# Wide one-row projections, statistics by matmul, and an order by longest path in a two-layer decode kernel

## The chip, the cores and the metric

The kernel runs on one core of one Trainium2 chip. The metric is the device time of one execution in microseconds (us). A kernel is timed several times, beside runs of the kernel before on the same chip. Of the kernel before, three runs gave a median of 344.33 us (342.01 to 346.02).

A program on one core also has a slower state in some executions; a run over 1.5% above the fastest of the same kernel is called slow. A median is of all executions, the slow ones too. A ratio is the mean time of one kernel's fast runs over the mean of the other's fast runs of the same rounds, so it is not quite the ratio of the medians that stand beside it. Chips differ by about one per cent (the kernel before had medians of 343.6 to 347.5 us in the calls below), so runs of different calls are compared by their ratios.

In the profile, PE is TensorE (its matmuls), PEld its weight loads, DVE VectorE, ACT ScalarE, POOL GpSimd and SP the engine that issues DMAs; "L439" is line 439 of that run's kernel file, so one place in the code has different numbers in different runs.

## The reference

Eight rows (the batch), one token each, width 448. Two layers, each an attention over the last 1,024 keys of a cache (16 query heads, 8 key/value heads, 256 wide) and an MLP (448 to 1,792 to 448). Both layers use the same cache and the same weights:

```
x = x + A(layernorm(x))      # q = x wq; softmax(q k^T / 16) v; wo
x = x + B(layernorm(x))      # silu(x w1) w2
x = x + A(layernorm(x))
x = x + B(layernorm(x))
```

## The kernel before

The weights stay in SBUF. The keys and values of one row are 16 loads of 512 KB (8.4 MB); they come into 27 slots and serve both layers of their row, so they are read once. A slot gets its next load when layer 2 of its row is done with it. The queries of layer 1 are made for all rows at the start, and the last MLP is done for all rows at the end. In between, each row goes through layer 1, its MLP and the scores of layer 2 on its own. The kernel is a list of tasks. A planner simulates them and fixes the order of each engine before the program is built:

```python
def push(t):                       # next task: smallest prio given by hand
    heapq.heappush(heap, ((t.prio if t.eng != "sp" else -1e9), t.idx, t))
...
def proj(bank_i, col, outs, ins, lhs, rhs, n, fresh=True):    # all projections; one row: n == 1
    for o in outs:
        for i in ins:
            fns.append(lambda e, o=o, i=i: e.matmul(
                bank[bank_i][:, col + (o - outs[0]) * n:col + (o - outs[0] + 1) * n], lhs(o, i), rhs(i), ...))
...
def pv_cols(b, layer, kvh, ...):   # p times V, by columns of V: 16 matmuls into one bank
    c0 = DH + 4 * j
    ... e.matmul(bank[ob][:, c0 + 2 * a:c0 + 2 * a + 2], vs[...], pT_sb[...])
    dve(... oT_dst <- bank[ob][:, c0:c0 + 4] * rl_sb ...)     # DVE reads that bank
...
def layer1(b):
    # 16 DVE transposes of keys, scores, softmax, then by turns pv_rows / pv_cols and wo_part
def layer2(b):
    # chain(b): w1, silu, w2, statistics, wq;  then scores, softmax, pv_rows of layer 2
```

`[...]` and `...` are cuts.

## Time and profile before

The median is 344.33 us; the profiled execution has a span of 343.4 us. The next lines are from its page: busy time by engine, then the span in 40 slices (one digit is the busy share in tenths; PEclk is the granted TensorE clock in tenths of full speed), the DMA queues (packets, MB, share of the 16 engines), the chain of waits (SPq is the sequencer of SP, which issues the loads), and two groups of instructions (count, busy us, mean ns of one, then the idle time of the engine before them and what ended it).

```profile
PE 232.8 (68%) x5966; PEld 173.1 (50%) x5966; DVE 169.6 (49%) x510; ACT 46.4 (14%) x163; POOL 10.5 (3%) x22
...
PE   1052435677488886796779668777877688887584
...
PEclk9999999998555556559655965686568555655565
DMA  7999999999950699049925991799089808100000
...
q1 hardware_dynamic: 49936, 77.68, 66.0%
q8 instruction: 47, 0.77, 0.9%
...
PE 51%; DVE 13%; SPq 12%; DMA 9%; issue 8%; ACT 7%; DVEq 0%; ACTq 0%
...
L439 PE MATMUL bank<-oT,wo_sb 128*128 128x1 bf16 (+1 forms) x1152 | 32.2, 165 | 4.5 <-issue 4.5
...
L630 PE MATMUL bank<-pT_sb,slot 128*128 128x2 bf16 x512 | 17.6, 164 | 11.9 <-DVE oT L636 7.7
```

The reader is to see four things. No engine is full, so the time is a chain of waits, of which PE is half. After the first quarter PE runs at half clock for about three quarters of the time (mean clock 0.62 over 100 to 280 us). (The trace has no clock records of about the first 80 us; the 9s there are a filling and not a measurement: 64 score matmuls at 76.5 us take 3.58 us, as long as in half-clock stretches.) DMA pauses between rows, so the loads are not the limit. And "issue" is 8% of the chain: time for which the profile shows no cause. About half of it is stops in which PE stood still for 0.4 to 3.0 us; the rest is in pieces below 0.3 us. The stops stand beside packets of the queue named "instruction".

The row is the unit in what follows. I measure it from the start of a row's w2 projection to that of the next row. In the windows view, a line is the window, its length, the busy time of each engine, the clock, the DMA share and GB/s. Two rows of the kernel before:

```profile
142.34:175.22 32.88, 25.53 (x688) 19.39 (x688) 20.90 (x59) 5.22 (x19) 1.23 (x2) 0.66 0.73 258
...
208.09:241.87 33.78, 26.11 (x687) 19.59 (x688) 19.46 (x58) 5.32 (x19) 1.23 (x2) 0.65 0.70 251
```

From the timeline of PE (start, duration, instruction group):

```profile
178.01 1.42 PE L439 MATMUL bank<-xbt,wq_sb 112*128 112x1 bf16 x48
...
180.54 1.88 PE L543 MATMUL bank<-slot,qbd 128*8 128x256 bf16 x32
```

48 one-column matmuls take 1.42 us, 30 ns each with the pipeline's own latency of some 0.15 us in it; the 32 score matmuls take 1.88 us here, at half clock. At full clock they take 1.04 to 1.10 us.

### The profile page before, as it was taken

The numbers are of one execution on the slowest core, as the hardware profiler recorded it, in microseconds if no ns is written. First come the engines' busy times: TensorE is split into PE (matmuls) and PEld (weight loads), VectorE is DVE, ScalarE is ACT, GpSimd is POOL, SyncE is SP. The second block draws the span as 40 slices with busy tenths as digits, with TensorE's granted clock in tenths as the row PEclk, the third lists the DMA queues.
The fourth block names the chain that finished last, engine by engine and source line by source line (L and its number), as shares of the span: only waits on it lengthen the run. The fifth ranks groups of instructions, "written<-read, shape, count | busy, mean of one in ns | idle before, by whom it ended". The sixth has DMA issues, their size and how long they took to land.

```text
span 343.4 us, 12913 instructions
## 1 busy us (share of the span) xinstructions
PE 232.8 (68%) x5966; PEld 173.1 (50%) x5966; DVE 169.6 (49%) x510; ACT 46.4 (14%) x163; POOL 10.5 (3%) x22
## 2 busy tenths in 40 slices
PE   1052435677488886796779668777877688887584
PEld 0051125654277545664755466456654665476363
DVE  5069200467656644565647556635663566212313
ACT  2000000201102020203020302121112111211111
POOL 0001000000000100001000000100010000000000
PEclk9999999998555556559655965686568555655565
DMA  7999999999950699049925991799089808100000
GB/s 200 263 407 379 361 312 271 403 339 368 404 165 4 211 388 371 19 132 380 389 89 188 388 380 31 252 398 333 5 274 403 307 4 261 49 4 4 0 4 3
DMA packets 49989, 78.50 MB, mean 229 GB/s; under 512 B 2176, under 2 KB 40848, under 8 KB 49488
## 3 DMA queue, kind: packets, MB, share of 16 engines
q1 hardware_dynamic: 49936, 77.68, 66.0%
q8 instruction: 47, 0.77, 0.9%
q14 instruction: 6, 0.05, 0.0%
HBM read 77.67 MB, written 0.01 MB: 226 GB/s over the span
## 4 chain that ended last, share of the span: by engine, by line
PE 51%; DVE 13%; SPq 12%; DMA 9%; issue 8%; ACT 7%; DVEq 0%; ACTq 0%
PE bank L439 22%; PE bank L543 11%; PE bank L602 8%; SPq L417 7%; DMA slot<-in_A_k_cache_dram 5%; DMA w_sb<-in_B_w_dram 4%; PE bank L630 4%; SPq L405 2%; ACT e_sb L566 2%; SPq L411 2%; ACT o_sb L609 2%; DVE mseg L552 1%; PE bank L571 1%; DVE slot L782 1%; PE bank L522 1%
## 5 line engine op out<-in xcount | busy, mean ns | idle before, releaser
L782 DVE STREAM_TRANSPOSE slot<-slot 128x512 uint32<-128x512 uint32 x128 | 87.4, 698 | 13.9 <-DMA slot<-in_A_k_cache_dram 11.9
L543 PE MATMUL bank<-slot,qbd 128*8 128x256 bf16 x1024 | 58.9, 401 | 13.1 <-DVE slot L782 8.8
L543 PEld LDWEIGHTS bank<-slot,qbd 128*8 128x8 bf16 x1024 | 28.9, 113 | 30.4 <-DVE slot L782 9.5
L602 PE MATMUL bank<-slot,pT_sb 128*2 128x256 bf16 x768 | 36.4, 347 | 3.5 <-DMA slot<-in_A_v_cache_dram 3.5
L439 PE MATMUL bank<-oT,wo_sb 128*128 128x1 bf16 (+1 forms) x1152 | 32.2, 165 | 4.5 <-issue 4.5
L439 PEld LDWEIGHTS bank<-oT,wo_sb 128*128 128x128 bf16 x1152 | 31.4, 103 | 4.7 <-issue 4.7
L439 PE MATMUL bank<-xbt,wq_sb 112*128 112x1 bf16 x1024 | 32.1, 165 | 2.1 <-ACT xbt L695 2.1
L439 PEld LDWEIGHTS bank<-xbt,wq_sb 112*128 112x128 bf16 x1024 | 29.8, 104 | 6.2 <-issue 3.4
L630 PE MATMUL bank<-pT_sb,slot 128*128 128x2 bf16 x512 | 17.6, 164 | 11.9 <-DVE oT L636 7.7
L602 PEld LDWEIGHTS bank<-slot,pT_sb 128*2 128x2 bf16 x768 | 18.8, 99 | 12.8 <-DMA slot<-in_A_v_cache_dram 5.2
L630 PEld LDWEIGHTS bank<-pT_sb,slot 128*128 128x128 bf16 x512 | 15.6, 99 | 13.5 <-issue 10.0
L439 PE MATMUL bank<-xbt,w_sb 112*128 112x1 bf16 (+1 forms) x504 | 16.4, 166 | 6.7 <-issue 4.3
L439 PEld LDWEIGHTS bank<-xbt,w_sb 112*128 112x128 bf16 x504 | 15.0, 104 | 7.6 <-issue 4.4
L571 PE MATMUL bank<-ident,e_sb 128*128 128x128 bf16 x64 | 7.8, 259 | 14.9 <-ACT e_sb L566 14.9
L552 DVE TENSOR_REDUCE mseg<-bank 128x2 f32<-128x512 f32 x16 | 11.0, 687 | 13.2 <-PE bank L543 13.0
L511 POOL TENSOR_TENSOR qbd<-q1s,mask 128x256 bf16<-128x256 bf16 x16 | 9.8, 612 | 244.5 <-PE bank L543 220.7
L439 PEld LDWEIGHTS bank<-hT,w_sb 128*128 128x128 bf16 x448 | 12.7, 104 | 7.9 <-DVE hT L688 7.0
L439 PE MATMUL bank<-hT,w_sb 128*128 128x1 bf16 x448 | 13.4, 165 | 4.7 <-DVE hT L688 4.3
L636 DVE TENSOR_TENSOR oT<-bank,rl_sb 128x4 bf16<-128x4 f32 x32 | 5.2, 162 | 22.0 <-PE bank L630 22.0
L615 DVE TENSOR_TENSOR oT<-bank,rl_sb 128x16 bf16<-128x16 f32 x24 | 4.9, 204 | 22.1 <-PE bank L611 21.5
L571 PEld LDWEIGHTS bank<-ident,e_sb 128*128 128x128 bf16 x64 | 4.4, 112 | 20.7 <-ACT e_sb L566 18.9
L609 ACT ACTIVATE o_sb<-bank 128x256 bf16<-128x256 f32 x24 | 9.2, 383 | 41.4 <-PE bank L602 41.4
(108 smaller groups left out, 156.8 us busy)
## 6 DMA issues: line engine op xcount, KB each, us to landing
slot<-in_A_k_cache_dram SPq DMA_DIRECT2D x64, 512.0 KB, 9.5
slot<-in_A_v_cache_dram SPq DMA_DIRECT2D x64, 512.0 KB, 7.8
wq_sb<-in_A_wq_dram SPq DMA_DIRECT2D x4, 896.0 KB, 10.7
wo_sb<-in_A_wo_dram SPq DMA_DIRECT2D x1, 3584.0 KB, 27.4
w_sb<-in_B_w_dram SPq DMA_DIRECT2D x2, 1568.0 KB, 16.3
qbd<-in_A_x_dram SPq DMA_DIRECT2D x1, 7.0 KB
out_dram<-e_sb SPq DMA_DIRECT2D x1, 7.0 KB
```

The source lines that it names most:

```text
L405: dma(lambda e: e.dma_start(slots[s][:, :].rearrange("p (u d) -> p u d", d=DH), A_k_cache[b, kvh, S0:SK, :].rearrange("(p u) d -> p u d", ...
L411: dma(lambda e: e.dma_start(slots[s][:, :].rearrange("v (q n) -> v q n", q=4), A_v_cache[b, g, S0:SK, :].rearrange("(q v uh) d -> v q (uh ...
L417: dma(lambda e: e.dma_start(slots[s][:, :].rearrange("v (j n) -> v j n", j=4), src.rearrange("j (v uh) d -> v j (uh d)", uh=2)), [("slot", ...
L439: fns.append(lambda e, o=o, i=i: e.matmul(bank[bank_i][:, col + (o - outs[0]) * n:col + (o - outs[0] + 1) * n], lhs(o, i), rhs(i), start=( ...
L511: add("pool", lambda e, k2=k2: e.tensor_tensor(qbd[0][:, 4 * k2:4 * k2 + 4, :, :].rearrange("p k c (q r) -> p (k c) q r", r=2), q1s[:, b, ...
L543: fns.append(lambda e, cb=cb, par=par, j=j, kvh=kvh, kv=kv: e.matmul(bank[sc][32 * j:32 * j + 8, k2 * 256:(k2 + 1) * 256], qbd[qi][:, kvh, ...
L552: dve(lambda e: e.tensor_reduce(mseg[ei][:, 0:2], bank[sc][:].rearrange("p (k n) -> p k n", k=2), AX.X, ALU.max, negate=True), bk(sc), [(" ...
L571: pe([lambda e, c=c: e.matmul(bank[lb][:].bitcast(BF16)[:, c * P:(c + 1) * P], e_sb[ei][:, c // 2, c % 2, :], ident[:, :], is_transpose=Tr ...
L602: fns.append(lambda e, q=q, uh=uh, j=j, vv=vv: e.matmul(bank[ob][32 * j:32 * j + 2, k2 * DH:(k2 + 1) * DH], pT_sb[ei][:, k2 * 2 + uh, j * ...
L609: act(lambda e: e.activation(o_sb[oi][:], bank[ob][:, k2 * DH:(k2 + 1) * DH], ACTF.Copy), bk(ob), [("o", oi)], 0.42, prio, "oev")
L630: fns.append(lambda e, a=a, q=q, uh=uh: e.matmul(bank[ob][:, c0 + 2 * a:c0 + 2 * a + 2], vs[:, (2 * q + uh) * DH + a * P:(2 * q + uh) * DH ...
L782: dve(lambda e, v=v: e.transpose(v, v), [("slot", s)], [("slot", s)], 0.68, prio, "KT")
```

## The change

There are three parts and some small ones.

1. Projections of one row move 32 equal columns instead of one (`broadcast_to`), so that TensorE looks busy to its clock control.
2. The sums for layernorm come from matmuls of the bf16 row with ones and with itself, instead of a DVE reduction, an ACT square and a split into two bf16 parts.
3. The order of each engine follows the longest path to the end instead of hand-given priorities, with measured durations and latencies. Softmax and PV of layer 2 then fill gaps of the next row's layer 1.
4. Small moves: three short operations go from DVE to ACT, and `pv_cols` alternates between two PSUM banks, so that PE need not wait until DVE has read the first one.

```diff
+PE_LAT = 0.13
+LOAD_MARGIN = 1.5
...
+        for t in reversed(sorted(tasks, key=lambda t: t.idx)):     # rank: longest path to the end
+            r = 0.0
+            for u in succ[t.idx]:
+                lat = 0.04 if t.eng == u.eng else (PE_LAT + 0.05 if t.eng == "pe" else 0.05)
+                r = max(r, u.rank + lat)
...
-            heapq.heappush(heap, ((t.prio if t.eng != "sp" else -1e9), t.idx, t))
+            heapq.heappush(heap, ((-t.rank if t.eng != "sp" else -1e9), t.idx, t))
...
+    CW = 32
...
+        wide = n == 1
+        n = CW if wide else n
...
-                    bank[bank_i][:, col + (o - outs[0]) * n:col + (o - outs[0] + 1) * n], lhs(o, i), rhs(i),
+                    bank[bank_i][:, col + (o - outs[0]) * n:col + (o - outs[0] + 1) * n], lhs(o, i),
+                    rhs(i).broadcast_to([rhs(i).shape[0], CW]) if wide else rhs(i),
...
-        c0 = DH + 4 * j
+        vb = ob if j % 2 == 0 else LB[layer]
+        c0 = (DH if j % 2 == 0 else C_Q) + 4 * j
...
     def stats1(prio):
-        dve(lambda e: e.tensor_reduce(st[0:CP, 0:1], xbt[0:CP, :], AX.X, ALU.add), ...)
-        act(lambda e: e.activation(junk[0:CP, :], xbt[0:CP, :], ACTF.Square, ..., accum_out=st[0:CP, 1:2]), ...)
-        ...                                          # copy and subtract: split into two bf16 parts
+        fns = [lambda e, c=c: e.matmul(s1, ones_b[0:CP, :], xbt[0:CP, c:c + 1], ...) for c in range(KC)]
+        fns += [lambda e, c=c: e.matmul(s2, xbt[0:CP, c:c + 1].broadcast_to([CP, P]), xbt[0:CP, c:c + 1], ...)
+                for c in range(KC)]
...
+        prio = 100 * b + 170                         # layer 2: softmax and PV
         softmax(b, 1, prio + 2, rs16[b % 2], [("rs16", b % 2)])
```

## The prediction

> **What bounds the kernel now.** The chain of waits gives TensorE 51% of the span, DVE 13%, "issue" 8%; DMA matters only in the head. In the timeline, hT of row 0 is ready at 65 us, of row 1 at 106, of row 7 at 310: the last six rows take 34.0 us each, and 33 us follow. K/V loads (8.4 MB a row at about 390 GB/s, 21.5 us) are not the limit there. A row is one serial chain: w2, wq, layer-2 scores, softmax, PV, then the next row's layer-1 softmax, PV, wo, w1. In it: 32 score or PV matmuls take 1.88 us in stretches at half clock and 1.04 us at full (timeline); layer-2 softmax and PV of row b sit before the layer-1 softmax of row b+1 (row 5: 256.4 to 261.2 us); and TensorE stops 1.4 to 3.0 us about once a row, each stop beside a 16,384-byte instruction packet (47 in the DMA queues).
>
> The Trainium skill, "TensorE: Matmul & The Clock Gate" (The HAM clock gate), says that the clock is half or full, decided by 3.4 us windows of activity. The clock records agree: only 0.5 and 1.0, 3413 ns steps. Counting moved columns per window, full clock follows windows with dense score/PV work (about 3,000 full-array columns); dense one-column projections (over 100 matmuls a window) are always followed by half clock.
>
> **What the change does.**
> 1. Projections move 32 columns. They are spaced 27 ns now (128 in 3.43 us), so 32 columns should fit at no cost even at half clock. About 368 a row add 11,800 columns; a row then has about 28,000, or 3,350 per window over 28 us: just above what seems needed. I expect full clock 65 to 80% of the steady time. The chain has about 3.7 us a row that halving the clock adds; I expect 1.3 us of it left.
> 2. Statistics by matmuls drop the DVE reduce and split and the ACT square, mostly hidden behind w1/wq; perhaps 0.3 us each.
> 3. The order: row b's layer-2 softmax and PV now fill gaps of row b+1's wo part. Removes about 4.7 us a row from the chain, gives back 0.8.
>
> Summing the new chain by hand with the trace's durations: 28.9 us a row at full clock, plus 1.3 for half clock, plus about 1.5 for instruction stops, is 31.7, against 34.0. Head: w1 and w2 land at 58.0 and 62.5 as before, hT of row 0 near 63. The first period falls most, 41 to about 29, because layer-1 scores of row 1 no longer wait behind layer-2 softmax and PV. Tail 33 to 30. 92 + 6*31.7 + 30 = 312. Estimate: 311 us, range 297 to 327. Chances: faster 0.94, same 0.05, slower 0.01.
>
> **What would show it.** Groups: projection matmuls still about 27 ns apart. Clock: above 0.65 over 100 to 300 us, against about 0.61. Timeline: hT to hT about 31.5 us; the pT transposes of layer 1 of row b+1 before those of layer 2 of row b. PV groups 1.04 us more often. Stops of 1.5 to 3 us beside instruction packets remain.
>
> **What would make it wrong.** Wide projections costing more than 27 ns; activity below the threshold, leaving half clock (about 325); instruction stops multiplying because the wo part has over 300 dense matmuls; DVE blocked by a key transpose waiting for a load. Or clock full nearly always and stops hidden: below 300.

## The result, and the profile after

The changed kernel is correct and took 330.31 us (329.66 to 331.38, four runs), beside 344.27 us for the kernel before (342.01 to 346.02). The ratio is 0.9601, with a 95% interval of 0.9539 to 0.9663. It is faster, as forecast, but 19 us slower than the estimate of 311, and above the range of 297 to 327. The same views of its profile:

```profile
PE 223.5 (68%) x6082; PEld 166.3 (50%) x6082; DVE 147.3 (45%) x426; ACT 50.7 (15%) x163; POOL 10.5 (3%) x22
...
PE   1052363675866759778759787979597779798583
...
PEclk9999999996975985779656975587769676996755
DMA  7999999999875596829871998298729881900000
...
q8 instruction: 47, 0.77, 0.9%
...
PE 48%; SPq 18%; DVE 12%; ACT 9%; issue 8%; DMA 4%; ACTq 0%
...
L453 PE MATMUL bank<-oT,wo_sb 128*128 128x32 bf16 (+1 forms) x1152 | 38.0, 180 | 3.5 <-issue 2.9
...
L645 PE MATMUL bank<-pT_sb,slot 128*128 128x2 bf16 x512 | 18.0, 164 | 5.5 <-issue 3.9
```

The clock did rise and the wait of `pv_cols` for DVE (7.7 us before, L630) is gone. But PE is still busy for only 68% of the span. Rows 1, 5 and 6 in the windows view:

```profile
100.89:134.87 33.98, 25.29 (x700) 18.55 (x700) 17.02 (x49) 5.80 (x19) 1.22 (x2) 0.75 0.69 230
...
234.88:268.78 33.90, 25.93 (x699) 18.67 (x700) 16.91 (x48) 5.80 (x19) 1.23 (x2) 0.75 0.71 240
268.78:297.83 29.05, 24.41 (x699) 18.36 (x700) 15.12 (x44) 5.80 (x19) 0.00 (x0) 0.83 0.42 137
```

Rows 1 to 5 take as long as before, 33 to 34 us; row 6 takes 29.05 us. Here is the forecast in its own parts, beside what the timeline shows:

| part | forecast, us | measured, us | difference |
|---|---|---|---|
| head, to w2 of row 0 | 63 | 63.8 | +0.8 |
| first period (row 0 to row 1) | about 29 | 37.1 | +8.1 |
| six periods | 6 x 31.7 = 190 | 196.9 | +6.7 |
| tail after the last | 30 | 31.8 | +1.8 |

The six periods hold five of 33.6 us on average, 1.9 us too long each, and row 6, 2.7 us shorter than forecast. What sets row 6 apart is that its loads end inside it (DMA share 0.42, no load left for a next row) and that no stop of PE above 0.3 us falls into it. The waits view of PE (line, what it waited for: us in total, times, longest) tells how much the stops grew. First the kernel before, then the one after; all lines that end in "issue" are shown:

```profile
PE bank L439 <- issue: 10.2, 6, 3.0
...
PE bank L543 <- issue: 2.3, 2, 1.6
```

```profile
PE bank L453 <- issue: 10.7, 8, 2.9
...
PE bank L645 <- issue: 3.9, 3, 1.8
...
PE bank L616 <- issue: 3.8, 2, 2.5
...
PE bank L557 <- issue: 2.6, 3, 1.6
...
PE bank L659 <- issue: 1.7, 1, 1.7
```

12.5 us in all before, 22.7 after. One such stop, from the timeline of PE in row 1:

```profile
120.34 0.60 PE L453 MATMUL bank<-oT,wo_sb 128*128 128x32 bf16 x18
...
123.80 0.27 PE L453 MATMUL bank<-oT,wo_sb 128*128 128x32 bf16 x4 [2.86 <-issue]
```

PE stops in the middle of one projection, whose inputs are all there, for 2.86 us. In the DMA records a packet of 16,384 bytes on the instruction queue starts at 121.32 us and takes 1.09 us; PE goes on 1.39 us after its end. This holds for every stop: the 17 of after and the 8 of before each end 1.27 to 1.60 us after such a packet has ended. Of the other waits of PE in these two traces (72 and 134), 2 and 6 end between 1.2 and 1.7 us after one. So what ends a stop is the arrival of instructions. Row by row, the stops of 0.5 us or more add up to 4.7 us in row 0 and 3.4, 4.3, 2.7, 2.3 and 3.3 us in rows 1 to 5, a mean of 3.2; the kernel before had 2.1 in the same rows. The forecast had put in 1.5.

The Trainium skill says where these packets come from ("Runtime: NRT & Kernel Launch", section "Instruction fetch mechanics"): instructions come in blocks of 16 KiB, 256 instructions, and the next block is fetched while the present one runs; the cost of crossing from block to block it calls "mostly hidden". The trace agrees on the size: 6,082 matmuls and 6,082 weight loads over 47 packets are 259 a packet. It does not agree that the cost is hidden: the stops above end when a block has come.

So the first theory was: the hand sum of the row is right, and what is missing are stops of TensorE for instructions, which come while K/V loads run. Rivals: the widened projections cost time after all; the new order is worth less than its 3.9 us a row; the new statistics lengthen the chain; the stops belong to certain instructions and not to block boundaries.

### The profile page after: what moved, and what is told of

It reads as the page before. It is cut to its first block, busy times and chain, and to the rows that moved or that the text cites. A ratio compares the mean times of both kernels' runs of the same rounds, so it can differ in the third digit from the quotient of the medians.

```text
span 329.6 us, 13056 instructions
## 1 busy us (share of the span) xinstructions
PE 223.5 (68%) x6082; PEld 166.3 (50%) x6082; DVE 147.3 (45%) x426; ACT 50.7 (15%) x163; POOL 10.5 (3%) x22
## 4 chain that ended last, share of the span: by engine, by line
PE 48%; SPq 18%; DVE 12%; ACT 9%; issue 8%; DMA 4%; ACTq 0%
PE bank L453 22%; PE bank L616 11%; PE bank L557 8%; SPq L429 7%; SPq L417 7%; DVE slot L795 5%; DMA slot<-in_A_k_cache_dram 4%; ACT e_sb L580 4%; PE bank L645 3%; PE bank L585 2%; DVE mseg L566 2%; SPq L423 1%; DVE qbd L540 1%; ACT o_sb L623 1%; PE bank L625 1%
## 5 line engine op out<-in xcount | busy, mean ns | idle before, releaser
L795 DVE STREAM_TRANSPOSE slot<-slot 128x512 uint32<-128x512 uint32 x128 | 80.4, 681 | 14.2 <-DMA slot<-in_A_k_cache_dram 14.2
L557 PE MATMUL bank<-slot,qbd 128*8 128x256 bf16 x1024 | 50.8, 346 | 20.4 <-DVE slot L795 10.1
L616 PE MATMUL bank<-slot,pT_sb 128*2 128x256 bf16 x768 | 40.2, 330 | 11.7 <-DMA slot<-in_A_v_cache_dram 4.4
L557 PEld LDWEIGHTS bank<-slot,qbd 128*8 128x8 bf16 x1024 | 25.2, 98 | 34.5 <-DVE slot L795 11.4
L453 PE MATMUL bank<-oT,wo_sb 128*128 128x32 bf16 (+1 forms) x1152 | 38.0, 180 | 3.5 <-issue 2.9
L453 PE MATMUL bank<-xbt,wq_sb 112*128 112x32 bf16 x1024 | 32.6, 186 | 6.6 <-issue 4.5
L616 PEld LDWEIGHTS bank<-slot,pT_sb 128*2 128x2 bf16 x768 | 14.9, 87 | 19.2 <-issue 10.4
L453 PE MATMUL bank<-hT,w_sb 128*128 128x32 bf16 x448 | 13.3, 187 | 13.7 <-DVE hT L701 13.7
L453 PE MATMUL bank<-xbt,w_sb 112*128 112x32 bf16 (+1 forms) x504 | 17.4, 181 | 3.9 <-issue 3.4
L453 PEld LDWEIGHTS bank<-hT,w_sb 128*128 128x128 bf16 x448 | 12.5, 103 | 14.5 <-DVE hT L701 14.5
L566 DVE TENSOR_REDUCE mseg<-bank 128x2 f32<-128x512 f32 x16 | 11.1, 692 | 17.9 <-PE bank L557 17.9
L580 ACT ACTIVATE e_sb<-bank,mb 128x256 bf16<-128x256 f32 x16 | 6.7, 470 | 75.2 <-DVE mb L573 75.2
```

The lines of the kernel that those rows point to most:

```text
L453: fns.append(lambda e, o=o, i=i: e.matmul(bank[bank_i][:, col + (o - outs[0]) * n:col + (o - outs[0] + 1) * n], lhs(o, i), rhs(i).broadcas ...
L557: fns.append(lambda e, cb=cb, par=par, j=j, kvh=kvh, kv=kv: e.matmul(bank[sc][32 * j:32 * j + 8, k2 * 256:(k2 + 1) * 256], qbd[qi][:, kvh, ...
L566: dve(lambda e: e.tensor_reduce(mseg[ei][:, 0:2], bank[sc][:].rearrange("p (k n) -> p k n", k=2), AX.X, ALU.max, negate=True), bk(sc), [(" ...
L580: act(lambda e, k2=k2: e.activation(e_sb[ei][:, k2, :, :].rearrange("p uh (jj ul) -> p uh jj ul", ul=4), bank[sc][:, k2 * 256:(k2 + 1) * 2 ...
L616: fns.append(lambda e, q=q, uh=uh, j=j, vv=vv: e.matmul(bank[ob][32 * j:32 * j + 2, k2 * DH:(k2 + 1) * DH], pT_sb[ei][:, k2 * 2 + uh, j * ...
L795: dve(lambda e, v=v: e.transpose(v, v), [("slot", s)], [("slot", s)], 0.7, prio, "KT")
```

## The experiments

Eighteen kernels ran. "After" means the changed kernel, "before" the one before it. The expectations name theories by letters: A is the prediction's own accounting, in which each part is worth what the prediction gave it; the other letters are the rivals, as each text puts them. Each of the 18 passed the comparison with the reference, also those that are wrong, which the tolerance doesn't notice.

### Taking the change apart

**The projections one column wide again.**

```diff
-    CW = 32
+    CW = 1
```

> The changed kernel with the projections moved back to 1 column; order, statistics and everything else as changed. Theory A (the wide projections did what they were costed for, and what is missing is elsewhere: stops of TensorE beside instruction packets): mean granted clock falls from 0.75 a row to 0.6 or less, each row gets 1.5 to 2 us longer, time about 341 to 344 us, stops as before. Rival B (the wide projections buy nothing, that is where the forecast gain is missing): same time within 2 us (329 to 332), whatever the clock does.

Measured: 341.04 us, ratio 0.9957 (0.9876 to 1.0039). The clock in rows 1 to 6 falls to 0.50 to 0.55; one of these rows, and the 48 projection matmuls of after that are read below:

```profile
170.45:204.06 33.61, 28.42 (x700) 19.77 (x700) 17.01 (x48) 5.80 (x19) 1.22 (x2) 0.55 0.73 243
```

```profile
278.04 1.40 PE L453 MATMUL bank<-xbt,wq_sb 112*128 112x32 bf16 x48
```

In the new kernel the wide projections are worth 11 to 12 of the 14 us (10.7 by the medians, (0.9957 - 0.9601) x 344.3 = 12.3 by the ratios). That the wide matmuls themselves are free is seen in the timelines: 48 of them take 1.40 us in row 6 of after (29 ns each), where 48 narrow ones took 1.42 us above. The stops were 14.5 us and not "as before" (22.7): that part of the expectation missed. The skill's "TensorE: Matmul & The Clock Gate", Part 1, subsection "Wait — 56ns, not 53.3ns?", states a floor of about 25 ns from start to start for small matmuls; this case shows 25 ns at full clock and 27 at half clock within long groups, at 1 as at 32 columns (medians of before, after and this run).

**The old order, with all else of the change.**

```diff
-SEM_LAT = {"pe": 0.05, ...}; PE_LAT = 0.13; LOAD_MARGIN = 1.5
+SEM_LAT = {"pe": 0.06, ...}; PE_LAT = 0.0; LOAD_MARGIN = 0.0
-    heapq.heappush(heap, ((-t.rank if t.eng != "sp" else -1e9), ...
+    heapq.heappush(heap, ((t.prio if t.eng != "sp" else -1e9), ...
-        prio = 100 * b + 170
```

> The changed kernel with the queue order by the old hand-given priorities and old latencies; wide projections and new statistics stay. Theory A (the order pays, about 4 us a row off the chain before stops): time 338 to 346 us, rows 2 to 6 about 33 to 35 us, layer-2 softmax before the next row's layer-1 softmax again. Rival C (the order gave back what it took, for instance by key transposes that wait for loads at the head of DVE's queue): 328 to 334 us.

Measured: 332.49 us, ratio 0.9697 (0.9618 to 0.9776). The order is worth about 1% of the time (0.9697 against 0.9601, with intervals that overlap), and nothing like the 3.9 us a row of the forecast. In the two traces it does not shorten the rows at all: the six periods average 31.7 us in the old order and 32.8 in the new one. What it wins lies elsewhere: w2 of row 0 starts at 63.8 us instead of 68.0, the first period is 37.1 us instead of 39.3, the tail 31.8 instead of 34.0. The stops of the old order were 17.6 us. The time is that of rival C; its reason, transposes that wait for loads, is not tested here. (The plan keeps the new durations of operations; only priorities, latencies and margin are old.)

**The old statistics in the new kernel.** The edit puts `stats1` and `stats8` of before back.

> The changed kernel with the statistics of before (reduce, square and split on DVE and ACT, two small matmuls). Costed at 0.3 us twice a row: 7 rows * 0.6 = 4 us slower, about 334 us. If the statistics by matmuls are worth nothing: 330 us.

Measured: 329.55 us, ratio 0.9606 (0.9536 to 0.9675). The new statistics are worth nothing that these runs can see.

**Wide projections alone in the kernel before.** The edit is the part of the diff on `CW`, with the outputs laid out 32 apart.

> The kernel before with only the projections widened to 32 columns. Theory A: clock of the rows rises from 0.61 to 0.7 or more, about 1.5 us a row saved, 332 to 337 us, instruction stops of 1.4 to 3 us once a row remain. Rival B (wide projections buy nothing): 342 to 346 us.

Measured: 342.63 us, ratio 0.9958 (0.9864 to 1.0052). The time is that of rival B. Alone, the part that was worth 11 us in the new kernel is worth almost nothing.

**One bank for `pv_cols` in the new kernel, and two banks in before with wide projections.**

```diff
 # in after
-        vb = ob if j % 2 == 0 else LB[layer]
-        c0 = (DH if j % 2 == 0 else C_Q) + 4 * j
+        vb = ob
+        c0 = DH + 4 * j
```

> The changed kernel with the four column-form PV groups of a row back in one PSUM bank, as before (the change lets every second one use the bank of layer 1's softmax sums). Found after the first runs: in the kernel before, each of these groups waits 0.35 us for DVE to read the last one; four a row are 1.4 us, 9 to 10 us over 7 rows. Theory F (this unnamed part of the change carries much of the gain in a row by priorities): in the long-path order other work fills these waits, so here it costs less, 1 to 6 us: 331 to 336 us. If it is worth nothing anywhere: 330 us.

> The kernel before with the wide projections and the column-form PV groups in two banks in turn, nothing else. Theory F: 1.4 us a row off the wide one (342.6 us): 331 to 336 us, close to the changed kernel in old order (332.5 us). If the gap between those two comes from the statistics or from copies moved to ACT: 340 to 344 us.

Measured: 332.02 us for the first, ratio 0.9585 (0.9511 to 0.966), and 339.15 us for the second, ratio 0.9694 (0.9597 to 0.9791; two fast runs, 334.73 and 338.49). The kernel before had 347.54 us, so the ratios count. In the new order a second bank brings nothing: with one bank, too, the trace has no wait of these matmuls for DVE, where before had 7.7 us. In the old order it makes the step from 0.9958 to 0.9694. That is the same as the new kernel in the old order (0.9697): wide projections and two banks are the whole gain there.

**Two banks alone in before.**

> Before, with the two PSUM banks of the column-wise PV alone (projections stay one column wide, old order). The PV groups waited 0.35 us each for DVE, four to a row. If that wait alone explains what the two banks brought beside wide projections (ratio 0.996 to 0.969), the ratio here is 0.965 to 0.980. If both are needed, because a row gets full clock only with wide projections and without pauses, the ratio is 0.985 to 1.005.

Measured: 340.52 us, ratio 0.9883 (0.9745 to 1.002), with only two fast runs. It lies nearer to the second expectation, but its interval reaches into the first one too. The product of the two parts alone is 0.9958 x 0.9883 = 0.984, and both together gave 0.969. That fits a gain that needs both, but the intervals are too wide to call it shown.

**Two knobs on the forecast's other terms:** 64 columns for wo and w2, to raise the clock further, and a wider margin for loads in the plan.

```diff
 # a_cx64
-        n = CW if wide else n
+        cw = CX if bank_i == XB and not fresh else CW      # CX = 64
+        n = cw if wide else n
 # a_margin6
-LOAD_MARGIN = 1.5
+LOAD_MARGIN = 6.0
```

> The changed kernel with wo and w2 moving 64 columns (wq and w1 stay at 32). At full clock 64 columns should still fit the 27 ns between matmuls, at half clock they need 53 ns. If the clock is held by moved columns in a window: granted clock of rows 1 to 5 rises from 0.74 to 0.85 or more and the time falls to 322 to 327 us. If the time at half clock doubles without raising the clock: 335 us or more.

> The changed kernel, planned with 6 us in place of 1.5 us of margin between a load and the key transposes that read it: the three transposes that stand among wo's copies in DVE's queue move behind w2's start. Rival C (transposes waiting for loads at the head of DVE's queue hold up wo): rows 1 to 5 get shorter by 0.5 us or more, 325 to 328 us. Theory A: no gain, 329 to 333 us, since eleven transposes then stand on the chain after w2.

Measured: 335.94 us, ratio 0.9663 (0.9602 to 0.9725), and 338.38 us, ratio 0.9655 (0.9553 to 0.9757). The 64 columns did raise the clock (0.834 in the profile, against 0.788) and did not make the kernel faster. They were not free: in this trace they stand 53 ns apart at half clock (27 at 32 columns) and 29 to 31 ns at full clock (25), and most of w2, 56 matmuls in a row's chain, ran at half clock. So the run does not tell what the rest of half clock is worth. The margin brought nothing that its two fast runs (333.14 and 337.36) show.

### The stops

**No K/V loads for rows 2 to 7.** Only 8 of the 128 partitions are loaded, so that every load is still issued, waited for and counted by the planner at its full size; the outputs are wrong. The order of all engines is unchanged.

```diff
+        if b >= 2:
+            dma(lambda e: e.dma_start(slots[s][0:8, :]..., A_k_cache[b, kvh, S0:SK, :]...[0:8]),
+                [("slot", s)], W * DH * 2, "slot%d" % s)
+            return
```

> The changed kernel, where the K and V loads of rows 2 to 7 bring only 8 of the 128 partitions (wrong result on purpose; same instructions and order, a sixteenth of the traffic from about 85 us on). Theory A (the missing time is stops of TensorE while its instructions are fetched behind K/V traffic): stops of 0.5 us and more vanish after 100 us, rows 1 to 6 take 29 to 30 us each as the last row does now (29.05), time 305 to 312 us. Rival D (the stops come from the dense matmul stream alone, whatever DMA does): rows stay at 33 us, 328 to 331 us.

> The kernel before with the same cut of the loads of rows 2 to 7 (wrong result on purpose). Theory A: its stops (2.1 us a row in rows 1 to 5) vanish too, rows 1 to 6 at 31 to 33.5 us, time 330 to 336 us; the gap between the two kernels grows from 14 to 22 us or more, which is near what was predicted. Rival D: 342 to 345 us.

Measured: 312.33 us for after without loads, ratio 0.9098 (0.9004 to 0.9192), and 334.2 us for before without them, ratio 0.9735 (0.9637 to 0.9833). No stop of 0.5 us or more is left in either once row 1 is loaded; one of 0.16 us (after) and one of 0.41 us (before) are. All "issue" lines of the waits view, after without loads:

```profile
PE bank L463 <- issue: 2.0, 2, 1.8
...
PE bank L669 <- issue: 1.7, 1, 1.7
```

This is the 311 us of the forecast, almost, though the rows are longer than the 29 to 30 us that theory A gave them. Its six periods average 30.9 us, beside 28.9 + 1.3 = 30.2 in the hand sum without the stops. Against before without loads the change is worth 22 us (334.2 to 312.3); with loads it is worth 14. So a third of what the change wins is given back.

But no load also means that data is never late. The kept traces tell how much that can be: after 90 us DVE waits for keys for 1.1 us in all in after, and PE never for values, so there was hardly any late data to take away. And in the chain that ended last, stops of PE above 0.15 us make up 19.2 us in after and 0.2 us in after without loads, where the spans differ by 18.4 us (329.6 and 311.2). So on the chain the stops account for the difference; this is from one trace each.

**Keeping the traffic, but into a spare buffer.** Small loads carry the data, and the full loads go to three spare tiles which nobody reads.

> As a_noload, but for every small load of rows 2 to 7 a full 512 KB load of the same data goes to one of three scratch tiles that nothing reads (24 slots in place of 27 for room; wrong result on purpose). The traffic is there, the waits for data are nearly gone. Theory A: stops come back beside instruction packets, rows 1 to 5 at 32 to 34 us, time 322 to 330 us. Rival E (rows are slow because DVE and TensorE wait for late K and V data): as fast as a_noload.

Measured: 361.11 us, ratio 1.0519. It meets neither expectation. This run is inconclusive: the spare tiles left room for only 24 slots, and the planner counted the bytes twice, so the order of the engines changed as well. Stops beside instruction packets are back (2.77 us in one row), but the time says nothing.

**Moving the block boundaries.** 64 tiny matmuls in front of everything shift all later instructions within their blocks of 256.

```diff
+    pe([lambda e: e.matmul(bank[YB][0:1, 0:1], ones_b[0:1, 0:1], ones_b[0:1, 0:1], start=True, stop=True)] * 64,
+       ["ones_b"], bk(YB), 2.0, -20, "shift")
```

> The changed kernel with 64 tiny matmuls put in front, while TensorE waits for the first weights anyway: every later instruction stands 128 places further along, so the 16,384-byte instruction blocks end at other places of a row. Theory A: the stops move to other instructions (a stop in wo turns up in PV or w1), their sum a row stays within 2 to 4.5 us; time 326 to 334 us. If the stops belonged to certain instructions of the row, they would stay where they are.

Measured: 328.07 us, ratio 0.9543 (0.9463 to 0.9623), 21.6 us of stops. The stops move to other instructions: row 6, which had one of 0.27 us, now has two (2.25 us together). So they belong to the places of instruction blocks and not to what the instructions do.

**When the packets come.** The trace allows a count without a new run: how many TensorE instructions (matmuls and weight loads) start between one instruction packet and the next. The mean is 248 to 257 in every run, near the 256 of a packet. If each packet came in time, all distances would be about 256. I take the standard deviation over 100 to 285 us, in one trace each. Without loads it is 31 (before) and 32 (after). With them it is 98 and 127, and single packets come up to 544 instructions after the one before. The packet at 121.32 us, beside the stop of 2.86 us shown above, came 510 instructions after the one before: PE had run through two blocks, and stood until 1.39 us after this one had come. So under K/V traffic the packets come late, and a stop follows. The packets themselves take no longer: 1.06 us on average in after and 1.11 us without loads over the same stretch. What is late is their start. What remained open was which property of the traffic does it.

**Half the bytes, and fewer loads in flight.** In the first kernel each load of rows 2 to 7 fetches 64 of the 128 partitions. In the others every load of row 1 and later is complete, but SP waits before each one until the load two (or three, or four) before it has landed. The plan is left alone, so the order of all engines is the same as in after.

```diff
 # a_half: as a_noload above, [0:64] instead of [0:8]
 # a_pace2, a_pace3, a_pace4: in the code that emits the engines' programs; N is 2, 3, 4
+                    if e == "sp" and t.sem.startswith("slot"):
+                        seen.append(t)
+                        if len(seen) > 16 + N:
+                            o = seen[-1 - N]
+                            eng.wait_ge(handles[o.sem], o.val)
```

> After, but the K/V loads of rows 2 to 7 fetch 64 of the 128 partitions (outputs wrong on purpose; order of all engines unchanged). Without these loads the TensorE instruction packets came 256 instructions apart with a standard deviation of 32, and no stop followed; with them the deviation was 127 and the stops took 3.2 us a row. If the amount of traffic makes the packets late, half of it gives stops between none and 3.2 us a row, deviation 40 to 110, and 314 to 324 us. If any traffic is enough, 328 to 332. If what mattered in the run without loads was not traffic but data landing early, stops stay and the time is near 325.

> After, with one more wait in front of each K/V load from row 2 on: the load before the last has landed. So at most two 512 KB loads are in flight; order of all engines unchanged. If packets are late because many loads stand in the DMA engines at once, the deviation of the packet spacing falls below 90 and stops below 1.5 us a row, and the time falls to 318 to 326 unless loads then come late. If two loads keep the engines just as busy for a packet, stops stay at 2.5 to 3.5 us and the time is 328 to 336.

> As the run before with three loads in flight. If the number in flight counts, stops lie between those of two in flight and those of the changed kernel; if it does not, stops of 2.5 to 3.5 us a row and 327 to 333 us.

> After, with at most four 512 KB loads in flight (three gave a ratio of 0.9345, two 1.0447 because keys landed late, no limit 0.9601). If fewer loads in flight is what lets the instruction packets through, four lies between three and no limit: ratio 0.935 to 0.958. If three only happened to shift the stops to a harmless place, four may land anywhere, 0.93 to 0.97.

(The expectations say "from row 2 on" for the second; the wait begins after the first two, three or four loads of the second row, the one numbered 1 here.)

> Before, with at most three loads in flight. Its stops took 2.1 us a row over five rows; without loads it ran at a ratio of 0.9735. If pacing frees the instruction packets here too, the deviation of their spacing falls from 98 below 80 and the ratio is 0.970 to 0.990. If the gain needs the new order, 0.995 to 1.01.

Measured, with the stops ("issue" of PE in the waits view, all lines added up) and the deviation of the packet distance:

| kernel | us | ratio (95%) | stops, us | deviation |
|---|---|---|---|---|
| before | 344.27 | 1 | 12.5 | 98 |
| after | 330.31 | 0.9601 (0.9539 to 0.9663) | 22.7 | 127 |
| after, half the bytes | 320.48 | 0.9298 (0.9200 to 0.9397) | 13.2 (slow) | 86 (slow) |
| after, four in flight | 325.22 | two fast runs: 321.42, 322.47; by hand 0.938 | 13.5 | 119 |
| after, three in flight | 320.20 | 0.9345 (0.9264 to 0.9425) | 4.8 | 70 |
| after, two in flight | 356.39 | 1.0447 (1.0358 to 1.0536) | 1.5 | 50 |
| after, hardly any bytes | 312.33 | 0.9098 (0.9004 to 0.9192) | 3.7 | 32 |
| before, three in flight | 337.88 | 0.9764 (0.9643 to 0.9884) | 5.9 (slow) | 75 (slow) |
| before, hardly any bytes | 334.2 | 0.9735 (0.9637 to 0.9833) | 2.9 | 31 |

Stops and deviation are from one trace each, and two of these traces ("slow") fell in the slow state; a difference of a few microseconds between two sums means little (the kernel with the old statistics has 16.3 us of stops and the same time as after). The record calls the verdicts of these test kernels "unclear", and gives none for four in flight; but all four executions of three in flight (318.2 to 323.3 us) and both without loads (311.5 and 313.1) lie below all four of after (329.7 to 331.4).

Both theories of the traffic fit: with half the bytes there are fewer stops (in a slow trace; the two fast runs, 317.0 and 318.9 us, are faster too), and a limit on the loads in flight lowers them with all bytes moved. The stops fall with that limit step by step, 22.7, 13.5, 4.8 and 1.5 us. With two in flight the stops are nearly gone, but the loads then come late: in that run DVE waits for keys as in the first line below, and in the run with three as in the second (in after it is 14.2 us).

```profile
DVE slot L801 <- DMA slot<-in_A_k_cache_dram: 63.2, 26, 12.2
```

```profile
DVE slot L801 <- DMA slot<-in_A_k_cache_dram: 20.7, 13, 13.3
```

Three in flight is the balance here. It beats both kernels, and "issue" is 4% of its chain where it was 8%. All its "issue" lines in the waits view of PE:

```profile
PE bank L459 <- issue: 1.8, 2, 1.2
PE bank L665 <- issue: 1.2, 1, 1.2
PE bank L651 <- issue: 0.8, 1, 0.8
PE bank L622 <- issue: 0.8, 2, 0.4
PE bank L563 <- issue: 0.2, 1, 0.2
```

Its profile, with the DMA issues (size and median us from issue to landing) of after for comparison in the second fence:

```profile
PE   1042347375696968696979797968778878897583
...
PEclk9999999999598679876675879699697967865955
DMA  7999999979999698988986899599888895600000
...
slot<-in_A_k_cache_dram SPq DMA_DIRECT2D x64, 512.0 KB, 5.3
slot<-in_A_v_cache_dram SPq DMA_DIRECT2D x64, 512.0 KB, 5.4
```

```profile
slot<-in_A_k_cache_dram SPq DMA_DIRECT2D x64, 512.0 KB, 6.7
slot<-in_A_v_cache_dram SPq DMA_DIRECT2D x64, 512.0 KB, 6.3
```

The DMA line no longer falls to 0 to 2 between rows: the same bytes are spread out. In windows, two of its rows and all of its six periods' sum:

```profile
165.21:195.50 30.29, 25.61 (x700) 18.80 (x700) 16.91 (x48) 5.79 (x19) 1.22 (x2) 0.77 0.86 279
195.50:225.09 29.59, 23.94 (x700) 18.14 (x700) 16.96 (x48) 5.80 (x19) 1.23 (x2) 0.87 0.85 276
...
sum 184.10, PE 151.41 PEld 111.77 DVE 99.96 ACT 34.77 POOL 6.13; mean PE 25.23 PEld 18.63 DVE 16.66 ACT 5.79 POOL 1.02
```

184.1 us against 196.9 in after: 12.8 us less in the six periods. The forecast's own sum without stops was 6 x 30.2 = 181. Three in flight was not timed side by side with after; the two are compared by their ratios (0.9345 and 0.9601, whose intervals are apart).

## Why the prediction was wrong, point by point

**The direction was right, the size was not.** Faster was given 0.94, and it is faster; the estimate was 19 us too low.

**"Plus about 1.5 for instruction stops": this step failed.** The mechanism was named, but the term of the sum was mis-sized. It measured 3.2 us in rows 1 to 5 and 4.7 in row 0. The kernel before already had 2.1, and the prediction took less than that instead of more. Take the stops out, and the six periods of after are 196.9 - 16.2 = 180.7 us, beside the 181 of the forecast without stops. Why the stops grew is a reading: a late packet hurts only if PE would otherwise have worked, and in before PE often waited for DVE or ACT anyway. The sums fit that, 12.5 us in before, 14.5 with narrow projections, 17.6 in the old order, 22.7 in after, but each is of one trace, and no run took this by itself. The prediction's list of what would make it wrong had this very point, "instruction stops multiplying because the wo part has over 300 dense matmuls"; dense matmuls alone don't do it, since the same stream without loads has hardly any stop.

**"The first period falls most, 41 to about 29": this failed too.** It fell to 37.1. Stops of 4.7 us fell into it (the prediction does not say how much of its 29 was meant for stops). Beside them, row 1's keys are still arriving (the last one that its scores need lands at 73.9 us, 10 us into the period), and its scores ran at half clock (32 in 1.85 and in 1.88 us); what each of the two cost is not shown. In the run with hardly any bytes from row 2 on, this period was 32.4 us.

**"28.9 us a row at full clock, plus 1.3 for half clock": the sum was right, the split was not.** Row 6, with 0.3 us of stops, took 29.05 us. The rows of the run without loads averaged 30.9 us, and those with three loads in flight 30.7, beside 30.2. But the 1.3 us went with full clock for 65 to 80% of the time, and rows 1 to 5 had it for about half (next but one point). By the prediction's own 3.7 us that would leave about 2.0 us instead of 1.3, so a part of the agreement is luck.

**"32 columns should fit at no cost even at half clock": right.** Spacing stayed at 27 ns at half clock and 25 ns at full clock.

**"About 3,000 full-array columns" a window for full clock: right in direction, too high in result.** The clock of rows 1 to 5 rose from a mean of 0.63 to 0.74 (windows view). As the records hold only half and full, 0.74 is full clock for about half of the time; forecast was 65 to 80%. The Trainium skill, "TensorE: Matmul & The Clock Gate", Part 1: The HAM clock gate, gives two clock levels and windows of 3.4 us of activity; the records here hold only 0.5 and 1.0 and change in steps of 3,413 ns. It gives no measure of activity in columns. That came from the trace of before. Counted again there, the five windows of 3.4 us with 100 or more matmuls of one or two columns are all followed by half clock. The 11 windows that moved over 12,400 columns are all followed by full clock (score and PV matmuls stand four side by side in the array, so this is about 3,100 full-array columns); between 8,800 and 12,400 both occur. The narrow kernel (0.50 to 0.55 in its rows) fits that dense one-column matmuls don't count as busy.

**"Statistics ... perhaps 0.3 us each": wrong in size.** They are worth nothing measurable (0.9606 against 0.9601).

**"The order ... removes about 4.7 us a row ..., gives back 0.8": wrong.** The old order with everything else new is 1% slower, and in the traces its rows are shorter, not longer (31.7 against 32.8 us); the new order wins in the head, the first period and the tail. Part of what the prediction gave to the order may be PV work at half clock, which the wide projections also mend, and so have been counted twice; this is not shown.

**What the prediction left out:** the second bank of `pv_cols`. In the old order it and the wide projections make the whole gain (0.9694). In the new order it brings nothing (0.9585 without it): the wait is gone there with one bank too. The parts of this change are not additive: the wide projections are worth about 12 us in the new kernel and 1.4 us, within the noise, alone. That they work on the same waits of PE is my reading.

**What stays open:** on which DMA engine an instruction packet waits, and behind what, is not in the trace. The Trainium skill ("DMA: Bandwidth & Descriptors", section "Queues, rings and completion order") says that a DMA engine goes round-robin between the queues it has work for, one packet at a time. By that rule alone I would not expect the number of loads behind a queue to matter (this is my inference and not the page's), and it does here; no run here tells why. Nor is it worked out why three in flight removes 17.9 of 22.7 us of stops and wins only about 9 us by the ratios ((0.9601 - 0.9345) x 344.3). Some of it goes to late data: after 90 us DVE waits 4.9 us for keys there, and 1.1 us in after.

## What to carry to other kernels

When TensorE runs thousands of tiny instructions, its program is itself a stream from memory, and here it stood still for 22.7 us of 330, nearly all of it behind the kernel's own bulk loads; look for "issue" stops beside instruction packets, and limit how many bulk loads are in flight to what the consumers need (three of 512 KB here) before shortening the chain further. When a change has several parts, first ask which wait each part removes: parts that remove the same wait don't add up, and a denser chain may expose delays that waiting used to hide (the second is a reading, not shown).

## What the Trainium skill lacked or had wrong

- "Runtime: NRT & Kernel Launch", section "Instruction fetch mechanics", calls crossing a 16 KiB block "mostly hidden". Here TensorE stood 12.5 us (before) and 22.7 us (after) in stops that end 1.27 to 1.60 us after a block has come, up to 3.0 us each, and nearly all of it while bulk loads ran: 2.9 and 3.7 us with hardly any bytes from row 2 on, of which 0.4 and 0.2 us after row 1 was loaded.
- The same page has nothing on bulk loads in flight. No limit, four, three and two loads of 512 KB gave 22.7, 13.5, 4.8 and 1.5 us of stops, and the best time, 320.2 us, came with three.
- "DMA: Bandwidth & Descriptors", section "Queues, rings and completion order": the page gives the turn-taking by packet but no figure for how late a packet starts beside bulk loads. Here the distance of instruction packets had a deviation of 127 instructions with loads and of 32 without.
- "TensorE: Matmul & The Clock Gate", Part 1, has no measure of what counts as busy. Here dense one-column matmuls at 27 ns left the rows at a clock of 0.50 to 0.55; 32 equal columns at the same spacing gave about 0.74, and were free, while 64 were not (53 ns at half clock).
